# Output stores behind the next load, weight conversion in even steps, and a feed-forward activation moved to ScalarE

## The chip, the core and the metric

The kernel runs on one core of a Trainium2 chip. That core has TensorE (PE: matmuls, with PEld for its weight loads), VectorE (DVE), ScalarE (ACT), GpSimd (POOL) and SyncE (SP). SP here only issues transfers, and the core's 16 DMA engines carry them out. The metric is device time in microseconds (us), as a median of several runs; lower is better.

## The reference

Three stages follow each other: windowed attention over 4 x 8 heads of 576 positions, a mixture of 8 experts, and a feed-forward network. What the change touches belongs to the last one and to the preparation of its weights.

```python
def _moe_ref(x, w_gate, w1, w2):           # x is 2304 x 512, 8 experts, F = 1024
    ...                                    # P: gates, normalised by 8 rounds over rows and columns
    for e in range(E):
        h = np.maximum(x @ w1[e], 0.0)
        out += P[:, e:e + 1] * (h @ w2[e])

def _moe2_ref(x, w_in, w_out):             # d_ff = 2048
    h = x @ w_in
    g = np.where(h >= 1, h, np.where(h <= -1, 0.0, (h + 1) ** 2 / 4.0))
    return g @ w_out
```

The product weights w_in and w_out come as 64-bit numbers, which the kernel reads as pairs of 32-bit words and turns into fp32 itself.

## The kernel before

**Tiling.** The 2304 tokens are handled in three passes (k = 0, 1, 2) of 768 tokens. The inner width of experts and feed-forward is cut into units of 512 columns: units 0 to 15 for the experts (two an expert), 16 to 19 for the feed-forward. The main loop goes over a list of runs. A "u" run does one unit, first layer and plain second layer. An "e" run does two units, e = 4 to 7 in pass 1, e = 1 to 7 in pass 2, and e = 8 and 9, the feed-forward, in all three passes at the very end. Every fp32 product is three matmuls of high and low fp32r parts (L393).

**First layer (L398).** A 2x2 block product is done with seven block products (Strassen's scheme) in the order 1, 5, 6, 2, 7, 3, 4, each for two column groups q, so 14 steps of six matmuls. Steps 0 to 5 (blocks 1, 5, 6) are copied out of PSUM by ScalarE (L410); blocks 6 and 7 and 4 accumulate on the same bank `pa`, so block 6 waits until block 1 was copied, block 7 until the copy of block 6 is done, and block 4 until VectorE has added block 7 to its partner (L413). Each of the eight finished 128x384 tiles is given to an activation, which is a list of stages; one stage of every tile under way is issued a step.

**Second layer of an "e" run (L491).** Seven block products again, numbered n = 0 to 6 in the same order, 36 matmuls each in three steps (tiles 0, 2, 1). The sums and the high and low parts of the seven left operands are made by `Seven` while PE works, at places that the tables FIRST_WORK and SECOND_WORK give ("s" a sum, "h" a high part on ScalarE, "l" a low part on VectorE). The operands and their weights live in three buffers each, so the weights of n = 6 are loaded when n = 3 has been done with, and the next run's three first weights after n = 4, 5 and 6 (L1331 to L1336). After each step a `join` adds the product to `acc`; in the last run of each pass (e = 9) it also issues the store of a finished piece on SP, at once (L577).

**Conversion (double_steps, L212).** During passes 1 and 2 the 64-bit weights are converted in 32 pieces of 128x512: seven VectorE instructions a piece (L284 to L302, then L309 for w_in or L318 for w_out). For w_out each pair of pieces is split by `kept_pair` into high parts (ScalarE, L110), low parts (VectorE, L111) and four stores (L238); it is an iterator called `back`, advanced between the conversion's instructions by `advanced(back)`, and run to its end by `drain(back)` where its input is about to be overwritten. The parts go through two buffers called `raw2`, so a high part waits until the store two before has landed. `pull(double)` in the main loop issues one step of this generator. `at.hold` stops it before the scratch memory is needed for the next pass's input, and `at.held` says that it has stopped.

**Queues.** All transfers are issued by SP in the order of the program; an issue waits there for its semaphores, and everything behind it waits too. The program order on every engine is the order of the code.

Of the kernel before, what the change touches and what calls it, by code (L numbers as in the profile page):

```python
# [8 lines left out]
F32 = mybir.dt.float32  # L9
# [18 lines left out]
def tile_attention_moe_ffn(ctx: ExitStack, tc, q, k, v, w_gate, w1, w2, w_in, w_out, out):  # L28
# [183 lines left out]
    def double_steps(scr, stage1, stage2):  # L212
# [56 lines left out]
        for n, (u, m, c) in enumerate(pieces):  # L269
            while at.hold:  # L270
                loaded = -1
                at.held = True
                yield
            at.held = False
            if loaded < n:
                load(n)
                for _ in range(8):
                    yield
            loaded = n
            if n + 1 < len(pieces) and not at.hold:  # L280
                loaded = n + 1
                load(n + 1)
            w0, w1_ = (raws[n % 2].rearrange("p (f w) -> p f w", w=2)[:, :, i] for i in range(2))
            nc.vector.tensor_scalar(out=ai, in0=w1_, scalar1=0x7FFFFFFF, scalar2=None, op0=ALU.bitwise_and)  # L284
            yield
            nc.vector.tensor_scalar(out=a, in0=a, scalar1=F64_LO, scalar2=F64_HI, op0=ALU.max, op1=ALU.min)
            if advanced(back):
                yield
            yield
            nc.vector.tensor_scalar(out=ai, in0=ai, scalar1=3, scalar2=0x3FFFFFF8,  # L290
                                    op0=ALU.logical_shift_left, op1=ALU.bitwise_and)
            yield
            nc.vector.scalar_tensor_tensor(out=ai, in0=w1_, scalar=-0x40000000, in1=ai,
                                           op0=ALU.bitwise_and, op1=ALU.bitwise_or)
            if advanced(back):
                yield
            yield
            nc.vector.tensor_scalar(out=ti, in0=ai, scalar1=-0x800000, scalar2=None, op0=ALU.bitwise_and)
            yield
            if advanced(back):  # L300
                yield
            nc.vector.scalar_tensor_tensor(out=t, in0=w0.bitcast(U32), scalar=2.0 ** -52, in1=t,  # L302
                                           op0=ALU.mult, op1=ALU.mult)
            yield
            if m == 0:
                if c == 0:
                    drain(back)
                    raw = stage1()
                nc.vector.tensor_tensor(out=raw[:, c, :], in0=a, in1=t, op=ALU.add)  # L309
                yield  # L310
                if c == KC - 1:
                    yield from prep_w1(u, raw, lambda i: stage2().bitcast(F32R).rearrange(
                        "p h (q c f) -> p h q c f", q=UQ, c=2), 2)
            else:
                if c == 0 and u % 2 == 0:
                    raw = stage1()
                pair = [raw[:, c % 2 * 2 + i, :] for i in range(2)]
                nc.vector.tensor_tensor(out=pair[u % 2], in0=a, in1=t, op=ALU.add)  # L318
                yield
                if u % 2:  # L320
                    drain(back)
                    back = kept_pair(u // 2, c, pair)
# [158 lines left out]
    def work(ops, what):  # L481
        for x in what.split():
            {"h": ops.hi, "l": ops.low, "s": ops.sum}[x[0]](int(x[1]), int(x[2]))

    FIRST_WORK_FFN = {1: "h10 h11", 3: "l10", 4: "l11", 5: "s50", 6: "s51 h50", 8: "h51", 12: "l50", 13: "l51"}
    SECOND_WORK_FFN = {(0, 1): "s60 s61 h60", (0, 2): "h61 l60 h20", (1, 0): "l61 h21",
                       (1, 1): "l20 l21", (1, 2): "s70 s71 h70", (2, 0): "h71 l70", (2, 1): "l71",
                       (2, 2): "h30 h31", (3, 0): "l30 s40", (3, 1): "l31 s41", (3, 2): "h40 h41", (4, 0): "l40",
                       (4, 1): "l41"}

    def seven_second(finish, buf, tag):  # L491

# [74 lines left out]
    def join_plain(e, k):  # L567

        def join(o, i, x, d):
            at_ = acc[:, x, d * HD:(d + 1) * HD]  # L570
            if e == E and i in (1, 5, 6, 4):
                nc.scalar.activation(out=at_, in_=o, func=AF.Copy)
                return
            nc.vector.tensor_tensor(out=at_, in0=o, in1=at_, op=ALU.add)
            if e == E + N_PAIR - 1 and i in (2, 7, 3, 4):
                t = k * TPP + x
                nc.sync.dma_start(out=out[t * P:(t + 1) * P, d * HD:(d + 1) * HD], in_=at_)  # L577
        return join

    def act_relu(src, f, j, h_=None):  # L580
        h_ = h_ or hs
# [356 lines left out]
    def advanced(steps):  # L938
        return next(steps, steps) is not steps
# [5 lines left out]
    with tc.manual_schedule():  # L945
# [113 lines left out]
        w2o = late.tile([P, 2, KC, DM], F32R, name="w2o")  # L1059
        half = late.tile([P, 1], F32, name="half")  # L1060
        nc.vector.memset(half, 0.5)
        unity = late.tile([P, 1], F32, name="unity")
        nc.vector.memset(unity, 1.0)

        def stage1():
            return late.tile([P, KC, UF], F32, tag="raw1", bufs=1, name="raw1")
# [51 lines left out]
                return [lambda: nc.scalar.activation(out=hid[:, half_, j, f], in_=src, func=AF.Relu)]  # L1118
            return act

        at.room, at.slot = None, 0

        def act_ffn(half_):
            def act(src, f, j):
                if at.room is None:
                    at.room = stage1().rearrange("p c f -> p (c f)")
                at.slot = (at.slot + 1) % 5
                r = at.room[:, at.slot * HALF:(at.slot + 1) * HALF]

                def clamp():  # L1130
                    if f % 2 and j:
                        nc.scalar.activation(out=r, in_=src, func=AF.Relu, bias=half, scale=0.5)
                        nc.scalar.activation(out=r, in_=r, func=AF.Relu, bias=unity, scale=-1.0)
                        nc.scalar.activation(out=r, in_=r, func=AF.Square, bias=unity, scale=-1.0)
                    else:
                        nc.vector.tensor_scalar(out=r, in0=src, scalar1=-1.0, scalar2=1.0, op0=ALU.max, op1=ALU.min)
                        nc.scalar.activation(out=r, in_=r, func=AF.Square, bias=half, scale=0.5)

                return [clamp, lambda: None, lambda: nc.vector.tensor_tensor(out=hid[:, half_, j, f], in0=r, in1=src, op=ALU.max)]
            return act  # L1140

        def turn_steps(k, more, tag):
# [46 lines left out]
        for n, run in enumerate(runs):  # L1189
# [138 lines left out]
            drain(nxt)  # L1328
            for n_, t in seven_second((join_scaled if moe else join_plain)(e, k), bufs, tags[0]):
                work(ops, second_work.get((n_, t), ""))  # L1330
                if t == TPH - 1:  # L1331
                    later = n_ + 3
                    if later < len(ORDER):
                        load_op(e, ORDER[later], words(w2_buf[(ring + later) % 3]))
                    elif after and after[0] == "e":
                        load_op(after[1], ORDER[later - 7], words(w2_buf[(ring + later) % 3]))  # L1336
                if not ends and (n_, t) >= (4, 0):
                    pull(double)
                if ends and (n_, t) in ((1, 2), (2, 2), (3, 2), (4, 1), (4, 2), (5, 0), (5, 1), (5, 2), (6, 0), (6, 1)):
                    pull(build)  # L1340
            left = build
            tags.reverse()
            ring = (ring + 7) % 3
# [32 lines left out]
```

## Time and profile before

| | |
|---|---|
| Median of 3 runs | 2015.83 us (2014.94 to 2017.61) |
| The profiled execution's own time | 2012.49 us |
| Its span, first to last instruction | 2010.6 us |
| PE busy | 1967.5 us (98%) |
| DVE busy | 1468.7 us (73%) |
| ACT busy | 964.9 us (48%) |
| POOL busy | 309.2 us (15%) |
| DMA, mean over the span | 265 GB/s |

The profiled execution took 1.9 us more than its span, and 3.34 us less than the median of the runs. PE's share is an average over the whole program; what a wait costs is read where it stands. In the trace's rows a time is counted from the span's start, the second number is the duration, and a bracket at the end gives how long the engine stood idle before the row and who ended that.

### The profile page before, as it was taken

To read this page: it belongs to the slowest core of one execution; us is meant where nothing else is said; L and a number is where in the kernel's file an instruction comes from. 1 tells how busy PE (TensorE), PEld (TensorE's weight loads), DVE (VectorE), ACT (ScalarE), POOL (GpSimd) and SP (SyncE) were. 2 spreads that over 40 slices of the span, in tenths; PEclk is the share of its full clock that TensorE was granted. 3 is DMA by queue.
4 is the path that set the end of the run, shared out by engine and by line. 5 is a ranking of instruction groups with operands and counts; after the bars stand their busy time and mean duration, and the time that the engine had idled before them with its cause. 6 is when DMAs were issued, how large, how long until landed. Compare 5 with 4: busy or idle time off the path is not lost.

```text
span 2010.6 us, 33603 instructions
## 1 busy us (share of the span) xinstructions
PE 1967.5 (98%) x12602; PEld 1863.0 (93%) x12602; DVE 1468.7 (73%) x2640; ACT 964.9 (48%) x2089; POOL 309.2 (15%) x327
## 2 busy tenths in 40 slices
PE   8999999999999999999989999999999999999998
PEld 7887879898998989988989999999999999999998
DVE  6644587889988867767766576777887576986867
ACT  6555445555554443323444344444454455565554
POOL 4212214534435401011000001000000000000000
PEclk9999999999999999999999999999999999999999
DMA  7423467987788887778877868888788867787773
GB/s 177 109 67 100 180 237 279 344 312 298 297 319 315 330 308 285 280 278 309 293 272 262 278 235 331 316 284 291 291 320 320 313 248 284 241 295 267 263 250 127
DMA packets 234866, 533.07 MB, mean 265 GB/s; under 512 B 80848, under 2 KB 128464, under 8 KB 214992
## 3 DMA queue, kind: packets, MB, share of 16 engines
q1 hardware_dynamic: 234704, 530.92, 74.8%
q8 instruction: 100, 1.64, 0.3%
q14 instruction: 62, 0.51, 0.1%
HBM read 374.10 MB, written 156.76 MB: 264 GB/s over the span
## 4 chain that ended last, share of the span: by engine, by line
PE 88%; DVE 6%; DMA 3%; ACT 2%; issue 1%; SPq 0%; ACTq 0%; DVEq 0%
PE pa L395 21%; PE py L395 20%; PE pc L395 10%; PE qy L395 7%; PE qh L395 7%; PE qt L395 6%; PE pb L395 5%; PE ph L395 3%; PE qs L395 2%; PE s L747 2%; PE qx L395 1%; PE px L789 1%; PE pt L715 1%; PE pe L773 1%; DVE xf L368 1%; DMA w_sums<-raw 1%
## 5 line engine op out<-in xcount | busy, mean ns | idle before, releaser
L395 PE MATMUL pa<-xo,w1o 128*128 128x384 f32 x2736 | 516.5, 337 | 12.7 <-DVE kept L413 10.0
L395 PEld LDWEIGHTS pa<-xo,w1o 128*128 128x128 f32 x2736 | 479.4, 189 | 17.3 <-DVE kept L413 12.4
L395 PE MATMUL py<-w2o,hh 128*128 128x512 f32 x1104 | 341.6, 391 | 0.0
L395 PE MATMUL pc<-xo,w1o 128*128 128x384 f32 x1368 | 257.5, 335 | 1.8 <-DVE w1o L111 1.2
L137 POOL TENSOR_TENSOR raw<-raw 128x256 f32<-128x256 f32 x152 | 139.9, 948 | 755.1 <-DVE raw L111 275.1
L410 ACT ACTIVATE kept<-pa 128x384 f32<-128x384 f32 x228 | 110.6, 490 | 287.6 <-PE pa L395 286.6
L395 PEld LDWEIGHTS py<-w2o,hh 128*128 128x128 f32 x1104 | 207.5, 188 | 41.2
L395 PEld LDWEIGHTS pc<-xo,w1o 128*128 128x128 f32 x1368 | 238.9, 188 | 2.4 <-DVE w1o L111 1.5
L395 PE MATMUL py<-w2o,hl 128*128 128x512 f32 x552 | 215.3, 390 | 0.0
L368 DVE TENSOR_TENSOR xf<-xf 128x768 f32<-128x768 f32 x156 | 145.2, 958 | 0.8
L413 DVE TENSOR_TENSOR kept<-pb,kept 128x384 f32<-128x384 f32 x114 | 62.7, 555 | 109.3 <-PE pb L395 108.3
L111 DVE TENSOR_TENSOR w1o<-raw,w1o 128x256 fp32r<-128x256 f32 x210 | 127.7, 656 | 13.6 <-ACT w1o L110 13.3
L395 PE MATMUL pb<-xo,w1o 128*128 128x384 f32 x684 | 128.9, 335 | 0.0
L395 PEld LDWEIGHTS py<-w2o,hl 128*128 128x128 f32 x552 | 104.1, 189 | 21.7
L111 DVE TENSOR_TENSOR third<-xf,third 128x768 fp32r<-128x768 f32 (+1 forms) x110 | 105.8, 971 | 22.5 <-ACT third L110 22.3
L584 ACT ACTIVATE hh<-kept 128x384 fp32r<-128x384 f32 x138 | 72.4, 525 | 98.6 <-DVE kept L413 98.5
L395 PEld LDWEIGHTS pb<-xo,w1o 128*128 128x128 f32 x684 | 119.1, 188 | 0.0
L110 ACT ACTIVATE third<-xf 128x768 fp32r<-128x768 f32 (+1 forms) x110 | 83.9, 786 | 68.5 <-DVE xf L368 18.8
L110 ACT ACTIVATE w1o<-raw 128x256 fp32r<-128x256 f32 x210 | 77.3, 414 | 67.2 <-POOL raw L137 67.2
L1118 ACT ACTIVATE xf<-kept 128x384 f32<-128x384 f32 x132 | 67.6, 523 | 64.2 <-DVE kept L413 63.7
L585 DVE SCALAR_TENSOR_TENSOR hl<-kept,hh 128x384 fp32r<-128x384 f32 x138 | 89.6, 652 | 6.2 <-ACT hh L584 4.4
L607 DVE SCALAR_TENSOR_TENSOR acc<-py,prob,acc 128x512 f32<-128x512 f32 x120 | 84.1, 740 | 11.2 <-PE py L395 11.2
(195 smaller groups left out, 3336.7 us busy)
## 6 DMA issues: line engine op xcount, KB each, us to landing
w1o<-w_kept SPq DMA_DIRECT2D x294, 512.0 KB, 5.7
w_kept<-w1o SPq DMA_DIRECT2D x105, 512.0 KB, 4.0
w2o<-w_sums SPq DMA_DIRECT2D x48, 1024.0 KB, 5.0
w2o<-w_kept SPq DMA_DIRECT2D x46, 1024.0 KB, 5.1
w_kept<-w2o SPq DMA_DIRECT2D x26, 1024.0 KB, 7.2
w2x<-w_kept SPq DMA_DIRECT2D x21, 1024.0 KB, 4.8
w2x<-w_sums SPq DMA_DIRECT2D x20, 1024.0 KB, 4.8
w_kept<-raw SPq DMA_DIRECT2D x36, 512.0 KB, 4.5
```

Source lines behind the costliest of these rows:

```text
L110: nc.scalar.activation(out=hi, in_=raw, func=AF.Copy)
L111: return lambda: nc.vector.tensor_tensor(out=lo, in0=raw, in1=hi.bitcast(F32), op=ALU.subtract)
L137: nc.gpsimd.tensor_tensor(out=out[:, q], in0=in0[:, q], in1=in1[:, q], op=op)
L368: nc.vector.tensor_tensor(out=dst, in0=in0, in1=in1, op=ALU.subtract)
L395: nc.tensor.matmul(o, lhsT=a(h), rhs=b(l), start=first and n == 0, stop=last and n == 2, skip_group_check=on)
L410: nc.scalar.activation(out=dst, in_=src, func=AF.Copy)
L413: nc.vector.tensor_tensor(out=dst, in0=src, in1=dst, op=ALU.add)
L584: return [lambda: nc.scalar.activation(out=hi, in_=src, func=AF.Relu), lambda: nc.vector.scalar_tensor_tensor(out=lo, in0=src, scalar=0.0, ...
L585: lambda: nc.vector.scalar_tensor_tensor(out=lo, in0=src, scalar=0.0, in1=hi.bitcast(F32), op0=ALU.max, op1=ALU.subtract)]
L607: nc.vector.scalar_tensor_tensor(out=o, in0=py, scalar=prob[:, t, e:e + 1], in1=o, op0=ALU.mult, op1=ALU.add)
L747: nc.tensor.matmul(s[:, i, :], lhsT=qd[:, pr, j, :], rhs=kt[:, pr, key0(j):key0(j) + KW], start=not early, stop=not early or i == JG - 1)
L1118: return [lambda: nc.scalar.activation(out=hid[:, half_, j, f], in_=src, func=AF.Relu)]
```

## The change

Four things are changed together.

1. `join_plain` no longer issues the store of a finished output piece; it writes it down, and `send_out` issues the stores that were written down after step 1 of each of the seven products, and once at the end of the run.
2. In `double_steps` the iterator `back` is advanced at four places of a piece instead of three, each time with a step of its own, `drain(back)` before a w_in piece becomes `yield from back`, and `at.held` is set as soon as a piece has been written. In pass 2 the generator is pulled from n = 3 on instead of n = 4.
3. The feed-forward activation was, for six of eight tiles, a clamp on VectorE and a Square on ScalarE, and for two of eight three instructions on ScalarE, then a maximum on VectorE. It becomes Relu and Square on ScalarE for all eight, and one VectorE instruction with minimum and maximum.
4. The tables FIRST_WORK_FFN and SECOND_WORK_FFN place the feed-forward's sums and parts at other steps.

```diff
@@ double_steps
             nc.vector.tensor_scalar(out=ai, in0=w1_, scalar1=0x7FFFFFFF, scalar2=None, op0=ALU.bitwise_and)
+            if advanced(back):
+                yield
             yield
...
             if m == 0:
                 if c == 0:
-                    drain(back)
+                    yield from back
                     raw = stage1()
                 nc.vector.tensor_tensor(out=raw[:, c, :], in0=a, in1=t, op=ALU.add)
+                at.held = at.hold
                 yield
...
-    FIRST_WORK_FFN = {1: "h10 h11", 3: "l10", 4: "l11", 5: "s50", 6: "s51 h50", 8: "h51", 12: "l50", 13: "l51"}
+    FIRST_WORK_FFN = {1: "h10 h11", 2: "l10 l11", 3: "s50", 4: "s51 h50 h51", 6: "l50", 7: "l51"}
...
@@ join_plain
             if e == E + N_PAIR - 1 and i in (2, 7, 3, 4):
-                t = k * TPP + x
-                nc.sync.dma_start(out=out[t * P:(t + 1) * P, d * HD:(d + 1) * HD], in_=at_)
+                at.done.append((k * TPP + x, d, at_))
         return join
+
+    def send_out():
+        for t, d, from_ in at.done:
+            nc.sync.dma_start(out=out[t * P:(t + 1) * P, d * HD:(d + 1) * HD], in_=from_)
+        at.done.clear()
...
@@ act_ffn
-                def clamp():
-                    if f % 2 and j:
-                        nc.scalar.activation(out=r, in_=src, func=AF.Relu, bias=half, scale=0.5)
-                        nc.scalar.activation(out=r, in_=r, func=AF.Relu, bias=unity, scale=-1.0)
-                        nc.scalar.activation(out=r, in_=r, func=AF.Square, bias=unity, scale=-1.0)
-                    else:
-                        nc.vector.tensor_scalar(out=r, in0=src, scalar1=-1.0, scalar2=1.0, op0=ALU.max, op1=ALU.min)
-                        nc.scalar.activation(out=r, in_=r, func=AF.Square, bias=half, scale=0.5)
-
-                return [clamp, lambda: None, lambda: nc.vector.tensor_tensor(out=hid[:, half_, j, f], in0=r, in1=src, op=ALU.max)]
+                def squared():
+                    nc.scalar.activation(out=r, in_=src, func=AF.Relu, bias=half, scale=0.5)
+                    nc.scalar.activation(out=r, in_=r, func=AF.Square)
+
+                return [squared, lambda: None,
+                        lambda: nc.vector.scalar_tensor_tensor(out=hid[:, half_, j, f], in0=r, scalar=1.0, in1=src,
+                                                               op0=ALU.min, op1=ALU.max)]
...
@@ main loop, second layer of an "e" run
                 work(ops, second_work.get((n_, t), ""))
+                if t == 1:
+                    send_out()
                 if t == TPH - 1:
                     later = n_ + 3
...
-                if not ends and (n_, t) >= (4, 0):
+                if not ends and n_ >= (4 if k < 2 else 3):
                     pull(double)
...
+            send_out()
             left = build
```

Three places show how the order moves. The first is VectorE's program around the border of pass 1's runs e = 4 and e = 5 and the first layer of e = 5: L111 on `raw` is a low part of the conversion, L309 the first w_in piece, L413 the first layer's addition. Before:

```order
L563 SCALAR_TENSOR_TENSOR acc<-qh,prob,acc 128x256 x3
L290 TENSOR_SCALAR xf<-xf 128x512
L293 SCALAR_TENSOR_TENSOR xf<-xf 128x512
L111 TENSOR_TENSOR raw_9711<-raw_8672,raw_9711 128x2x256
L298 TENSOR_SCALAR xf<-xf 128x512
L302 SCALAR_TENSOR_TENSOR xf<-xf 128x512
L111 TENSOR_TENSOR raw_9788<-raw_8672,raw_9788 128x256
L111 TENSOR_TENSOR raw_9812<-raw_8672,raw_9812 128x2x256
L111 TENSOR_TENSOR raw_9816<-raw_8672,raw_9816 128x2x256
L309 TENSOR_TENSOR raw_9820<-xf 128x512
L413 TENSOR_TENSOR kept_9748<-pb_9744,kept_9748 128x384
L413 TENSOR_TENSOR kept_9749<-pb_9745,kept_9749 128x384
```

With the change, at the same place of PE's order (L566 is the join that was L563, L417 the addition that was L413):

```order
L566 SCALAR_TENSOR_TENSOR acc<-qh,prob,acc 128x256 x3
L302 TENSOR_SCALAR xf<-xf 128x512
L304 SCALAR_TENSOR_TENSOR xf<-xf 128x512
L321 TENSOR_TENSOR raw_8670<-xf 128x512
L284 TENSOR_SCALAR xf<-xf 128x512
L288 TENSOR_SCALAR xf<-xf 128x512
L111 TENSOR_TENSOR raw_9770<-raw_8670,raw_9770 128x2x256
L417 TENSOR_TENSOR kept_9738<-pb_9734,kept_9738 128x384
L417 TENSOR_TENSOR kept_9739<-pb_9735,kept_9739 128x384
```

Three low parts in a row, each behind a high part that waits for a buffer, and L309 stood ahead of the additions; one low part is left there, and the others follow in later steps.

The second is SP's program at the border of pass 1's last "u" run and e = 4: L238 is a store of converted weights, L263 a load of raw 64-bit weights, L188 the loads of second-layer weights for e = 4, L171 those of first-layer weights. Before:

```order
L238 DMA w_sums_128<-raw_9082 128x2x512
L238 DMA w_sums_128<-raw_9110 128x2x512
L263 DMA xf<-in_moe_w_out_dram 128x1024
L238 DMA w_kept_118<-raw_9120 128x2x512
L188 DMA w2x<-w_kept_109 128x2048
L188 DMA w2o<-w_sums_124 128x2048 x2
L171 DMA w1o_70<-w_kept_90 128x1024
```

With the change:

```order
L238 DMA w_sums_128<-raw_9074 128x2x512
L238 DMA w_sums_128<-raw_9094 128x2x512
L263 DMA xf<-in_moe_w_out_dram 128x1024
L188 DMA w2x<-w_kept_109 128x2048
L188 DMA w2o<-w_sums_124 128x2048 x2
L171 DMA w1o_70<-w_kept_90 128x1024
L238 DMA w_kept_118<-raw_9129 128x2x512
```

The store that stood ahead of the three second-layer loads now stands behind them and behind one load of first-layer weights.

The third is SP's program in pass 0's run e = 9, at the products n = 3 to 5; L577 and L584 are the stores of finished output, the first L188 after them the load for n = 6. Before:

```order
L188 DMA w2o<-w_sums_129 128x2048
L577 DMA out_dram<-acc 128x256 x3
L188 DMA w2o<-w_kept_120 128x2048
L577 DMA out_dram<-acc 128x256 x3
L188 DMA w2x<-w_kept_117 128x2048
```

With the change:

```order
L188 DMA w2o<-w_sums_129 128x2048
L584 DMA out_dram<-acc 128x256 x2
L188 DMA w2o<-w_kept_120 128x2048
L584 DMA out_dram<-acc 128x256 x3
L188 DMA w2x<-w_kept_117 128x2048
```

The third store of n = 3 has moved behind the load for n = 6; the two stores before it are still ahead of that load.

## Rows read from the trace of the kernel before

**Rows 1.** Timeline of PE, 900 to 1060 us: start, us, what, [idle before, releaser]

```profile
917.82 2.36 PE L395 MATMUL pa<-xo,w1o 128*128 128x384 f32 x12 [1.87 <-DVE kept L413]
...
936.33 2.27 PE L395 MATMUL pa<-xo,w1o 128*128 128x384 f32 x12
...
953.71 3.71 PE L395 MATMUL pa<-xo,w1o 128*128 128x384 f32 x12 [2.63 <-DMA w1o<-w_kept]
957.22 2.52 PE L395 MATMUL pc<-xo,w1o 128*128 128x384 f32 x12
...
1019.16 5.99 PE L395 MATMUL pa<-xo,w1o 128*128 128x384 f32 x24 [6.37 <-DVE kept L413]
```

**Rows 2.** A window of 50 us: length, PE, PEld, DVE, ACT, POOL busy, granted clock, DMA

```profile
1000.00:1050.00 50.00, 43.63 (x276) 43.31 (x275) 30.26 (x50) 22.85 (x42) 2.22 (x3) 0.93 0.82 291
```

**Rows 3.** Chain of waits, 900 to 1060 us: start, us, what

```profile
907.22 8.34 DMA w_sums<-raw
...
1006.99 8.53 DMA w_kept<-raw
...
1015.63 0.64 ACT raw L110
...
1017.63 1.49 DVE kept L413 x3
```

**Rows 4.** Timeline of SP's issues, 930 to 960 us

```profile
940.37 0.36 SPq L238 DMA_DIRECT2D w_kept<-raw  x1
940.78 0.46 SPq L188 DMA_DIRECT2D w2x<-w_kept  x1
...
942.62 1.65 SPq L171 DMA_DIRECT2D w1o<-w_kept  x3
```

**Rows 5.** Timeline of PE in the feed-forward runs

```profile
1712.11 4.32 PE L395 MATMUL pa<-xo,w1o 128*128 128x384 f32 x24
...
1738.13 4.49 PE L395 MATMUL qh<-w2o,hh 128*128 128x256 f32 x34 [0.35 <-DVE hh L111]
...
1757.70 4.54 PE L395 MATMUL qh<-w2o,hl 128*128 128x256 f32 x36 [2.16 <-DMA w2o<-w_kept]
...
1879.77 5.87 PE L395 MATMUL qh<-w2o,hh 128*128 128x256 f32 x36 [2.42 <-DMA w2o<-w_kept]
...
2002.88 4.54 PE L395 MATMUL qh<-w2x,third 128*128 128x256 f32 x36 [2.10 <-DMA w2x<-w_kept]
```

**Rows 6.** Timelines of SP and of DVE in pass 0's run e = 9

```profile
1749.31 2.73 SPq L577 DMA_DIRECT2D out_dram<-acc  x3
1752.14 0.37 SPq L188 DMA_DIRECT2D w2o<-w_kept  x1
...
1748.87 0.75 DVE L574 TENSOR_TENSOR acc<-qs,acc 128x256 f32<-128x256 f32 x2
...
1751.27 0.41 DVE L574 TENSOR_TENSOR acc<-qx,acc 128x256 f32<-128x256 f32 x1
```

**Rows 7.** Groups by line, 1640 to 2011 us: count | busy, mean ns | idle before

```profile
L1137 ACT ACTIVATE raw<-raw,half 128x384 f32<-128x384 f32 x72 | 42.9, 612 | 32.1 <-DVE raw L1136 31.1
L110 ACT ACTIVATE hh<-xf 128x768 fp32r<-128x768 f32 x28 | 22.9, 841 | 17.0 <-DVE xf L368 12.2 <-PE qh L395 3.4 <-PE qx L395 1.2
L410 ACT ACTIVATE kept<-pa 128x384 f32<-128x384 f32 x47 | 22.2, 488 | 24.3 <-PE pa L395 24.3
L1132 ACT ACTIVATE raw<-kept,half 128x384 f32<-128x384 f32 x24 | 14.5, 605 | 2.3 <-DVE kept L413 2.2
...
L1139 DVE TENSOR_TENSOR xf<-raw,kept 128x384 f32<-128x384 f32 x72 | 39.6, 551 | 6.7 <-ACT raw L1134 6.5
...
L1136 DVE TENSOR_SCALAR raw<-kept 128x384 f32<-128x384 f32 x48 | 17.3, 360 | 1.7
```

**Rows 8.** Timeline of ACT in pass 0's run e = 9

```profile
1725.54 0.62 ACT L1133 ACTIVATE raw<-raw,unity 128x384 f32<-128x384 f32 x1
1726.19 0.62 ACT L1134 ACTIVATE raw<-raw,unity 128x384 f32<-128x384 f32 x1
```

More of the change, by code (lines that the diff above doesn't have):

```diff
@@ L291, in double_steps @@
                                     op0=ALU.logical_shift_left, op1=ALU.bitwise_and)
+            if advanced(back):
+                yield
             yield
@@ L299, in double_steps @@
             yield
-            if advanced(back):
-                yield
             nc.vector.scalar_tensor_tensor(out=t, in0=w0.bitcast(U32), scalar=2.0 ** -52, in1=t,
@@ L318, in double_steps @@
                 nc.vector.tensor_tensor(out=pair[u % 2], in0=a, in1=t, op=ALU.add)
+                at.held = at.hold
                 yield
@@ L483, in work @@
             {"h": ops.hi, "l": ops.low, "s": ops.sum}[x[0]](int(x[1]), int(x[2]))
-    FIRST_WORK_FFN = {1: "h10 h11", 3: "l10", 4: "l11", 5: "s50", 6: "s51 h50", 8: "h51", 12: "l50", 13: "l51"}
[L486 to L489, printed above, removed]
+    FIRST_WORK_FFN = {1: "h10 h11", 2: "l10 l11", 3: "s50", 4: "s51 h50 h51", 6: "l50", 7: "l51"}
+    SECOND_WORK_FFN = {(0, 0): "s60 s61 h60 h61", (0, 1): "l60 l61", (1, 0): "h20 h21", (1, 1): "l20 l21",
+                       (1, 2): "s70", (2, 0): "s71 h70 h71", (2, 1): "l70 l71", (3, 0): "h30 h31",
+                       (3, 1): "l30 l31", (3, 2): "s40", (4, 0): "s41 h40 h41", (4, 1): "l40 l41"}
     def seven_second(finish, buf, tag):
@@ L1061, in tile_attention_moe_ffn @@
         nc.vector.memset(half, 0.5)
-        unity = late.tile([P, 1], F32, name="unity")
-        nc.vector.memset(unity, 1.0)
         def stage1():
@@ L1119, in act_kept @@
             return act
-        at.room, at.slot = None, 0
+        at.room, at.slot, at.done = None, 0, []
         def act_ffn(half_):
```

## The prediction

> **What bounds the kernel.** I read four views in this order: the page's busy shares, the timeline of PE in stretches of 60 us (only rows with idle time ahead of them), the chain of waits around the longest of these, and the timelines of SP and DVE at the same places. PE is busy 98% of the span. So the time is PE's own work, which the change leaves as it is, plus the places where PE waits. After the first 280 us, in attention and the gates, which the change doesn't reach, there are few. In pass 1 there are three [rows 1]: 1.87 us and 6.37 us for VectorE's addition `kept`, and 2.63 us for first-layer weights. In the feed-forward each of the three e = 9 runs has one of 2.16, 2.42 or 2.10 us for the weights of n = 6, and one of about 0.35 us for a low part ahead of n = 2 [rows 5], of which one of three is shown.
>
> A wait costs more than its idle time where the clock falls after it. Twelve matmuls take 2.27 us at 936, but 3.71 and 2.52 us just behind the wait of 2.63; twenty-four take 4.32 us, but 5.99 us behind that of 6.37 [rows 1, 5]. The granted clock of the window with this wait is 0.93, and PE works 43.63 of its 50 us [rows 2], so part of it ran at 1.2 instead of 2.4 GHz. Behind 2.42 us the 36 matmuls took 5.87 us; behind 2.16 us they took 4.54 [rows 5].
>
> **The change part by part.** *Conversion.* The wait of 6.37 us is made by the drained `back`. In the chain [rows 3] a store needs 8.53 us to land, only then does ScalarE write the next high part into that buffer (1015.63), then VectorE makes the low part, and only then come the additions (1017.63) for which PE waits. In the changed order one low part is left ahead of the additions, its high part was issued a step before, and the store whose buffer it takes stands a product earlier in the run, over 10 us before. So the wait goes: 6.37 + (5.99 - 4.32) = 8.0 us. The 1.87 us at 917.82 [rows 1] have the same cause, with a store that took 8.34 us to land [rows 3] while two steps of `back` met at one place; now each has its own, and the buffer's store is issued some 6 us ahead of the high part: 1.9 us.
>
> What is late next? All conversion instructions remain, but low parts now stand between the conversion's steps. At the border of the last "u" run and e = 4 four high parts follow stores that are only 6 to 8 us older (PE's time between the two places). If such a store lands after 8.3 to 8.5 us, as those of [rows 3] did, instead of soon enough, VectorE is held 1 to 2 us. An addition has some 3 us before PE misses it: three steps of six matmuls lie between, and four such steps take 4.32 us [rows 5]. I take nothing, and keep 4 us for it as a bound: two such waits of 1.9.
>
> *The weights at 953.71.* SP issued the store of a low part at 940.37, then the second-layer loads from 940.78, and the first-layer load for which PE waited at 942.62 [rows 4]; it took 11.1 us to land, behind three megabytes. PE was done with the buffers of the second-layer weights when e = 4 began, at 936.33 [rows 1]. In the change that store stands behind these loads. The raw load ahead of them waits only for a conversion instruction which, by its place, VectorE does by about 936 (an estimate). So the loads start some 4 us earlier, and the first-layer load, which waits for PE's first block, is issued at 936.33 + 2.27 = 938.6 and, with the same 11.1 us, lands by 949.7, while PE needs it 14 steps after 936.33, at about 951. That gains 2.63 + 1.44 + 0.25 (what the two slow rows have over 2.27) = 4.3 us. Were the loads no earlier, the gain would be nothing.
>
> *Stores.* In the e = 9 run the third store waited for VectorE's join of qx, which ended at 1751.7, and the load for n = 6 was issued at 1752.14 [rows 6]; PE waited for it until 1757.70. In the change the load stands behind the two stores of qs alone, whose joins ended at 1749.6. That alone makes it 2.1 us earlier, just about the wait. VectorE is also less late by then: the second layer has six clamps of 0.36 to 0.55 us fewer ahead of it (L1136), and two low parts and two sums of the old order stand behind those joins now. I take 4 us earlier in all, so that the wait goes in all three passes: 2.16 + 2.42 + 2.10 + (5.87 - 4.54) = 8.0 us. The earlier parts of n = 2 take the waits of 0.35: 1.0 us.
>
> *Activation.* VectorE's part of a tile is one instruction of a maximum's size, 0.551 us [rows 7], as before, and the clamp is gone. ScalarE gets two instructions for each of eight tiles. The first is L1132's form, 605 ns. A dependent one starts 0.65 us after it [rows 8]. The second, a Square without a bias tile, isn't in the trace; it lies between a Copy without one (L410, 488 ns) and a Square with one (L1137, 612 ns). A tile then costs ScalarE 0.65 + 0.4 = 1.05 us with the overlap that neighbours show, 1.14 without it, and 1.26 with the long Square. I take 1.1, nearest to the Copy, whose operands are alike.
>
> The Trainium skill, "ScalarE: Activation LUTs", section "What ACT_TABLE_LOAD costs", gives 186 ns + 0.833 ns a column for immediates and 93 ns more for a bias tile; by that estimate the Square takes 506 ns and a tile 1.06 us.
>
> Over the two first layers of a run ScalarE then has 16 x 1.1 tiles, 12 copies of 0.49 and up to 7 high parts of 0.84 us [rows 7], 29.4 us, and PE 28 steps, which at a quarter of 4.32 us less the overlap of rows are some 29.1 us. That is level, so ScalarE ends a few us late, where the second layer leaves it room. The narrow place is the second copy of block 6: it now stands behind both high parts of operand 5, which wait for VectorE's sums. By adding the durations in order it ends 0.1 to 0.8 us before PE wants to add block 7. With 1.26 us a tile it would be up to 1 us late in each of six runs. I take 0.5 us in all, from nothing to 6 us.
>
> *Nothing else pays.* The end of the program keeps one store behind the last join. The conversion ends within pass 2's e = 6 as before, so no drain comes due. Pass 2 shows no wait of a microsecond, and three more instructions in n = 3 lie beside PE's 36 matmuls there.
>
> Sum: 8.0 + 1.9 + 4.3 + 8.0 + 1.0 - 0.5 = 22.7 us. The profiled execution took 2012.49 us (span 2010.6 and 1.9 around it) and would take 1989.8; the median of the runs is 3.34 us above it, so 1993.
>
> **Rivals.** *The loads stay late.* If VectorE's lag in e = 9 or the DMA queues make the loads as late as before, the 4.3 and 8.0 us stay: 1993 + 12.3 = 2005, or with one of the two about 2000. For it: the wait is cured by 2.1 us from the order alone, and a load of 1 MB needs 5.4 us or more with stores around it. Against it: VectorE's work ahead is less.
>
> *Store landings hold the spread conversion.* The waits of 1.9 and 6.4 us come back at the new places as two to four of 2 us each, one with a slow clock: about 8 us, 2001. For it: landings of 8.3 and 8.5 us. Against it: these two fell where several stores were in flight together.
>
> *ScalarE becomes the bound of the feed-forward (slower).* If a tile costs p us there, two first layers cost 16p + 11.8 us. The gain of 23 us is gone when each of six runs loses 3.9 us, that is from p = 1.32 on if nothing of the lag is absorbed, and at p = 1.6 six runs lose 8.3 us each: 1993 + 50 = 2043, slower than before. Against it: p over 1.26 needs waits that no row shows, and the second layer absorbs some us a run. The Trainium skill, same page, section "Rules for kernel authors", gives maximum and minimum to VectorE and not ScalarE; the clamp's 0.36 us against 0.605 us for the Relu that takes its place agrees.
>
> *No change.* The waits turn up elsewhere in full, since no engine's work falls by much: within 4 us of 2015.8. For it: PE is held by two slower engines in turn. Against it: both are idle a quarter of the time or more where PE waits.
>
> **How the numbers follow.** The forecast has 0.58, the late loads 0.16, the landings 0.12, ScalarE 0.06, no change 0.08. The best case adds the wait of 0.6 us in pass 2 and the pipeline's gap at each wait, some 3 us: 1990. For the upper end I take late loads with some of the landings: 2007. This holds about 0.8. The forecast's own range is 1989 to 1999. Four us, 0.2%, is what can be told from no change. Faster: 0.58 + 0.16 + 0.12, less 0.01: 0.85; same 0.09; slower 0.06.
>
> **What would show it.** Right: PE's rows at the first layers of pass 1's e = 4 and e = 5 and its last "u" run have no idle time over 0.5 us, the granted clock of that stretch is 1.00, n = 6 in each e = 9 run starts without a wait, ScalarE's Square takes about 0.5 us and no wait of PE names `kept` L414, the copy. Wrong: a wait of PE for ScalarE in the feed-forward, or for `kept` behind a low part of the conversion, or the load of n = 6 still landing behind PE.

## The result, and the profile after

The changed kernel takes 1985.33 us (median of four runs, 1984.10 to 1990.27), and the kernel before, on the same chip, 2016.72 (2014.94 to 2017.74). The ratio is 0.985, with a 95% interval of 0.9831 to 0.9869. The forecast was 1993 with a range of 1989 to 2007, so the direction was right and the gain too small: 31.4 us measured, 23 to 24 forecast.

The first and the fourth part of the page of the changed kernel: busy time of each engine, and the chain of waits.

```profile
PE 1957.6 (99%) x12602; PEld 1855.8 (94%) x12602; DVE 1436.8 (72%) x2567; ACT 982.9 (50%) x2137; POOL 312.5 (16%) x327
...
PE 94%; DVE 3%; ACT 2%; DMA 1%; issue 0%; SPq 0%; DVEq 0%; ACTq 0%
```

The three places of [rows 1] in the timeline of PE after the change:

```profile
915.91 2.24 PE L399 MATMUL pa<-xo,w1o 128*128 128x384 f32 x12
...
934.31 2.27 PE L399 MATMUL pa<-xo,w1o 128*128 128x384 f32 x12
...
946.81 4.61 PE L399 MATMUL pa<-xo,w1o 128*128 128x384 f32 x24
951.25 2.27 PE L399 MATMUL pc<-xo,w1o 128*128 128x384 f32 x12
...
1006.41 4.32 PE L399 MATMUL pa<-xo,w1o 128*128 128x384 f32 x24
```

None has idle time ahead of it, and 24 matmuls at 1006.41 take 4.32 us, where [rows 1] had 5.99 behind a wait of 6.37. The window of [rows 2] is full (same columns):

```profile
1000.00:1050.00 50.00, 50.00 (x360) 50.00 (x360) 36.69 (x59) 23.32 (x40) 1.43 (x2) 1.00 0.81 283
```

SP's issues ahead of e = 4, which answer to [rows 4]. Before, the store (L238) of 940.37 stood ahead of the second-layer loads (L188) and held them until 940.78, though the raw load (L263) had been issued at 936.48. Now they begin at 934.92, right behind the raw load, and the store stands behind them:

```profile
934.52 0.35 SPq L263 DMA_DIRECT2D xf<-in_moe_w_out_dram  x1
934.92 0.43 SPq L188 DMA_DIRECT2D w2x<-w_kept  x1
935.44 0.85 SPq L188 DMA_DIRECT2D w2o<-w_sums  x2
936.61 0.32 SPq L171 DMA_DIRECT2D w1o<-w_kept  x1
937.84 0.37 SPq L238 DMA_DIRECT2D w_kept<-raw  x1
```

In the feed-forward run e = 9 of pass 0, timelines of SP, DVE and PE (which answer to [rows 5, 6]): VectorE's joins of qs follow PE at once, the load for n = 6 is issued right behind their two stores, and PE starts n = 6 at 1738.14 with no wait. Nor is there a wait at n = 2 (1720.91), where [rows 5] had 0.35 us. What is left of idle time is 0.22 us in the next run, e = 8, and 0.21 in the e = 8 run after that, for a copy of ScalarE. SP, DVE and PE in this order:

```profile
1728.75 0.81 SPq L584 DMA_DIRECT2D out_dram<-acc  x2
1729.72 0.33 SPq L188 DMA_DIRECT2D w2o<-w_kept  x1
```

```profile
1728.30 0.76 DVE L577 TENSOR_TENSOR acc<-qs,acc 128x256 f32<-128x256 f32 x2 [0.28 <-PE qs L399]
```

```profile
1720.91 4.46 PE L399 MATMUL qh<-w2o,hh 128*128 128x256 f32 x36
...
1733.84 4.46 PE L399 MATMUL qt<-w2o,hh 128*128 128x256 f32 x36
1738.14 4.48 PE L399 MATMUL qh<-w2o,hl 128*128 128x256 f32 x36
...
1766.80 1.33 PE L399 MATMUL pa<-xo,w1o 128*128 128x384 f32 x6 [0.22 <-ACT kept L414]
```

ScalarE in the feed-forward, grouped by line (count, busy us, mean ns, idle before), and then one tile after another in its timeline. These answer to [rows 7, 8]:

```profile
L1137 ACT ACTIVATE raw<-raw 128x384 f32<-128x384 f32 x96 | 50.5, 526 | 3.0
L1136 ACT ACTIVATE raw<-kept,half 128x384 f32<-128x384 f32 x72 | 43.5, 605 | 8.3 <-DVE kept L417 7.9
```

```profile
1754.62 0.53 ACT L1137 ACTIVATE raw<-raw 128x384 f32<-128x384 f32 x1
1755.05 0.60 ACT L1136 ACTIVATE raw<-kept,half 128x384 f32<-128x384 f32 x1
1755.69 0.53 ACT L1137 ACTIVATE raw<-raw 128x384 f32<-128x384 f32 x1
1756.12 0.60 ACT L1136 ACTIVATE raw<-kept,half 128x384 f32<-128x384 f32 x1
```

A tile costs ScalarE 1.07 us (1755.05 to 1756.12), against 1.1 taken.

**Where the time went.** PE is the bound, so its time between the same matmuls of two kernels shows what a stretch gained. Two marks cut the span in three: PE's first product with `ident,acc` at about 717 us, and its first one after the passes. Before, then after:

```profile
716.67 0.38 PE L1150 MATMUL p<-ident,acc 128*128 128x128 f32 x2
...
1639.34 0.49 PE L1150 MATMUL p<-ident,acc 128*128 128x128 f32 x3
```

```profile
716.85 0.38 PE L1152 MATMUL p<-ident,acc 128*128 128x128 f32 x2
...
1622.78 0.49 PE L1152 MATMUL p<-ident,acc 128*128 128x128 f32 x3
```

With spans of 2010.6 and 1984.4 us the stretches are 716.67, 922.67 and 371.26 us before, and 716.85, 905.93 and 361.62 after: the passes gain 16.7, the feed-forward 9.6, the start nothing. Between the same matmuls inside the passes, the last "u" run of pass 1 gains 2.15, e = 4 4.2, e = 5 8.2 and pass 2 2.1.

### The profile page after: what moved, and what is told of

Its sections match the earlier page's. It is cut to its first block, busy times and chain, and to the rows that moved or that the text cites. A ratio compares the mean times of both kernels' runs of the same rounds, so it can differ in the third digit from the quotient of the medians.

```text
span 1984.4 us, 33637 instructions
## 1 busy us (share of the span) xinstructions
PE 1957.6 (99%) x12602; PEld 1855.8 (94%) x12602; DVE 1436.8 (72%) x2567; ACT 982.9 (50%) x2137; POOL 312.5 (16%) x327
## 4 chain that ended last, share of the span: by engine, by line
PE 94%; DVE 3%; ACT 2%; DMA 1%; issue 0%; SPq 0%; DVEq 0%; ACTq 0%
PE pa L399 22%; PE py L399 21%; PE pc L399 11%; PE qh L399 8%; PE qt L399 7%; PE qy L399 7%; PE pb L399 5%; PE ph L399 3%; PE qs L399 2%; PE s L754 2%; PE qx L399 1%; PE px L796 1%; PE pt L722 1%; PE pe L780 1%; PE pg L887 0%; DMA big<-in_q_dram 0%
## 5 line engine op out<-in xcount | busy, mean ns | idle before, releaser
L414 ACT ACTIVATE kept<-pa 128x384 f32<-128x384 f32 x228 | 110.8, 490 | 294.6 <-PE pa L399 293.5
L417 DVE TENSOR_TENSOR kept<-pb,kept 128x384 f32<-128x384 f32 x114 | 62.8, 556 | 105.4 <-PE pb L399 105.1
L111 DVE TENSOR_TENSOR w1o<-raw,w1o 128x256 fp32r<-128x256 f32 x210 | 117.6, 605 | 17.7 <-ACT w1o L110 17.5
L111 DVE TENSOR_TENSOR third<-xf,third 128x768 fp32r<-128x768 f32 (+1 forms) x110 | 101.2, 934 | 19.9 <-ACT third L110 19.8
L110 ACT ACTIVATE hh<-xf 128x768 fp32r<-128x768 f32 x78 | 63.3, 841 | 61.0 <-DVE xf L372 26.4
```

The source lines that it names most:

```text
L110: nc.scalar.activation(out=hi, in_=raw, func=AF.Copy)
L111: return lambda: nc.vector.tensor_tensor(out=lo, in0=raw, in1=hi.bitcast(F32), op=ALU.subtract)
L414: nc.scalar.activation(out=dst, in_=src, func=AF.Copy)
L417: nc.vector.tensor_tensor(out=dst, in0=src, in1=dst, op=ALU.add)
```

## The experiments

Twelve kernels, in three groups, each group on one chip beside runs of the kernel before (2015.33 to 2016.16 us). "Passes" and "feed-forward" are the stretches above, in each kernel's profiled execution.

| Kernel | median us | ratio, interval | start | passes | feed-forward |
|---|---|---|---|---|---|
| before, the first profile | 2015.83 | | 716.67 | 922.67 | 371.26 |
| before again (e4) | 2016.0 | 0.9994, 0.998 to 1.0007 | 723.58 | 924.94 | 373.38 |
| conversion alone (e1) | 1995.79 | 0.9891, 0.9876 to 0.9905 | 716.48 | 907.46 | 372.96 |
| stores alone (e2) | 2006.16 | 0.9949, 0.9936 to 0.9961 | 717.64 | 925.56 | 363.30 |
| activation and order (e3) | 2006.82 | 0.9951, 0.9936 to 0.9967 | 716.50 | 926.51 | 361.29 |
| order alone (e7) | 2006.41 | 0.9956, 0.994 to 0.9971 | 719.26 | 923.35 | 360.69 |
| activation alone (e10) | 2006.48 | 0.9952, 0.9935 to 0.9969 | 715.36 | 924.05 | 365.49 |
| stores, activation, order (e5) | 2003.19 | 0.9942, 0.9927 to 0.9957 | 719.04 | 926.82 | 361.34 |
| all three (after) | 1985.33 | 0.985, 0.9831 to 0.9869 | 716.85 | 905.93 | 361.62 |
| after, drain kept (e6) | 1985.95 | 0.9853, 0.9838 to 0.9868 | 716.54 | 908.05 | 361.61 |
| after, old activation (e9) | 1986.95 | 0.9853, 0.9837 to 0.987 | 717.36 | 905.91 | 361.13 |
| after, old stores (e11) | 1985.48 | 0.985, 0.9832 to 0.9869 | 714.87 | 906.18 | 361.75 |
| after, h51 later (e12) | 1986.14 | 0.9849, 0.9832 to 0.9865 | 715.66 | 908.07 | 360.67 |
| after, third ScalarE step (e8) | 2031.49 | 1.0086, 1.0057 to 1.0116 | 715.40 | 907.92 | 407.38 |

**The change in its parts.** e1 is the kernel before with the conversion's hunks of the diff (with `at.held` and the `pull` line), e2 with `send_out` and its calls, e3 with `squared` and both tables. e4 is the kernel before, unchanged.

> Of the four changes only the one to the conversion (back advanced evenly, at.held early, pass 2 pulled from n = 3). If the terms simply add, its trace loses the three waits of pass 1 (8.2, 4.3 and 2.1 us) and some 1.5 us in pass 2, and keeps the feed-forward's waits of 2.1 to 2.4 us: a ratio to the kernel before of 0.992 (16 us). If the runs of the kernel before lie 4 us above its first profile because its pass 1 waits vary, the gain in the runs is 19 to 21 us, 0.990. If the waits only move, it is under 8 us.

> Only the output stores are issued later. Theory: the order alone makes the load of n = 6 some 2.1 us earlier, so the waits of 2.1 to 2.4 us in the three e = 9 runs shrink to under 0.5 us and the clock drop behind one of them goes; the 0.35 us ahead of n = 2 stay: 6 to 8 us, ratio 0.9965. Rival: VectorE's lag sets the load's time and the stores of qs hold it as long: under 3 us, ratio 0.9985 or above.

> Only the activation and the two feed-forward tables. Theory: VectorE comes earlier to the joins, so the stores are released earlier and the load for n = 6 with them, though a store still stands ahead: the waits of 2.1 to 2.4 us shrink to 0.5 to 1.5 us, those of 0.35 us go, and 0.2 us come in for the copy L414 in the e = 8 runs: 3 to 6 us, ratio 0.998. Rival: all of the gain in the feed-forward comes from here (8 us, 0.996) or none (under 1 us).

> The kernel before, unchanged, for another execution's trace. If its executions differ by the waits of pass 1 and the feed-forward, its waits ahead of PE differ from 1.87, 2.63 and 6.37 us (pass 1) and 2.16, 2.42 and 2.10 us (feed-forward) by more than 1 us in sum, and a run with a longer span shows it there or in a lower clock; if they differ in attention, the first 280 us are longer or shorter by that much and the rest is the same.

The conversion alone gains 1.1%, or 20.4 us, and all of it in the passes. That is the second of e1's three texts, in which the runs of the kernel before lie above its first profile. Its waits at n = 6 stay, and one of 1.36 us for first-layer weights is left, as PE's timeline in e1 shows:

```profile
952.36 2.32 PE L399 MATMUL pc<-xo,w1o 128*128 128x384 f32 x12 [1.36 <-DMA w1o<-w_kept]
...
1742.34 5.90 PE L399 MATMUL qh<-w2o,hl 128*128 128x256 f32 x35 [2.22 <-DMA w2o<-w_kept]
```

Stores alone and activation with order alone each gain 0.5%, and all of it in the feed-forward. That is 10.0 and 9.3 us, more than either theory gave (6 to 8, and 3 to 6). Each takes away the same waits at n = 6. The kernel before, taken again, has the waits of the first profile in other sizes: 3.57, 2.15 and 6.68 us in pass 1, and 2.52, 2.47 and 2.23 at n = 6. Its start took 6.9 us longer as well. Its timeline of PE at e = 5:

```profile
1027.57 7.28 PE L395 MATMUL pa<-xo,w1o 128*128 128x384 f32 x24 [6.68 <-DVE kept L413]
```

**Do the gains in the feed-forward add up?** e5 is the changed kernel with the conversion's hunks undone. e11 undoes the stores alone:

```diff
-                at.done.append((k * TPP + x, d, at_))
+                t = k * TPP + x
+                nc.sync.dma_start(out=out[t * P:(t + 1) * P, d * HD:(d + 1) * HD], in_=at_)
...
-                if t == 1:
-                    send_out()
...
-            send_out()
```

> The changed kernel with the conversion's steps of before: stores behind the loads, the new activation and its order of parts stay. Theory (overlap): the stores and the activation each remove the same wait, that of the e = 9 runs for the weights of n = 6, so both together are worth what one is, 10 to 11 us: 2005 to 2007 us; pass 1 keeps waits of about 1.9 to 4, 2 to 2.6 and 5.5 to 6.7 us, and n = 6 has none. Rival (the gains add up): 2016.7 - 10.6 - 9.9 = 1996. Rival (the third part is worth what is left of the whole, 31.4 - 20.9): also 2006, which agrees with the first.

> The changed kernel with the output stores issued at the joins, ahead of the next load, as before. Theory (overlap: the order of the parts already lets the load land in time): no wait at n = 6, 1984 to 1988 us. Rival (the stores hold a share of the gain of their own): waits of 0.5 to 2 us at n = 6 and 1990 to 1995.

They don't. Stores and activation together gain 12.1 us (0.58%) and not the sum of some 19. The feed-forward takes 361.34 us, as with the activation and order alone, and with the old stores the whole change is as fast as with the new ones (e11). e5 keeps all three waits of pass 1:

```profile
922.12 3.67 PE L395 MATMUL pa<-xo,w1o 128*128 128x384 f32 x12 [3.81 <-DVE kept L413]
...
960.40 4.21 PE L395 MATMUL pa<-xo,w1o 128*128 128x384 f32 x12 [3.70 <-DMA w1o<-w_kept]
...
1025.89 6.68 PE L395 MATMUL pa<-xo,w1o 128*128 128x384 f32 x24 [5.46 <-DVE kept L413]
```

**Order or activation?** e7 is the kernel before with the two new tables FIRST_WORK_FFN and SECOND_WORK_FFN alone, e10 with `squared` alone, e9 the changed kernel with `clamp` in the place of `squared`.

> The kernel before with the two new tables alone, which say at which steps of a feed-forward run the high parts, low parts and sums are made. Theory (the removed clamps relieve VectorE): the three waits of 0.35 us ahead of n = 2 go, those of 2.1 to 2.5 us for the weights of n = 6 stay in two or three passes, at 1 to 2.5 us: 2012 to 2016. Rival (the order of the parts relieves VectorE at its joins): the waits at n = 6 go as well and the time is that of the activation with its tables, 2005 to 2008.

> The kernel before with the new activation alone, the order of the parts as before. Theory (either of the two relieves VectorE enough): no wait over 0.7 us at n = 6, the three of 0.35 us ahead of n = 2 stay, 2006 to 2010 us. Rival (the order does it all): the waits of 2.1 to 2.5 us at n = 6 stay, 2013 to 2017.

> The changed kernel with the activation of before (VectorE's clamps, or three ScalarE steps), the new order of parts, stores and conversion stay. Theory (the order of the parts, not the cheaper activation, relieves VectorE at the joins): 1984 to 1987 us as with the new activation, no wait at n = 6, and the waits of 0.2 us for the second copy of block 6 go, since ScalarE has less to do. Rival (the clamps make VectorE late again): waits of 0.5 us and more in the feed-forward, 1988 to 1995.

For e7 my theory fell: the order of the parts alone takes away every wait of the feed-forward, 360.69 us. In e10 neither text was right about the waits. Those at n = 6 shrink, to 1.65, 1.61 and 1.18 us, and those ahead of n = 2 go: 365.49 us. The medians (2006.48 and 2006.41 us) don't tell e10 from e7; only the traces do. In e9 the old activation with the new order gives 361.13 us, with no wait of 0.2 us in the feed-forward. So the order alone is enough, and with it the new activation adds nothing that the runs show.

What decides at n = 6 is when the load is issued against PE's start of the product before (qt). In [rows 6] the load is issued at 1752.14, 1.05 us after qt's start in the same profile, PE's timeline of before:

```profile
1751.09 4.46 PE L395 MATMUL qt<-w2o,hh 128*128 128x256 f32 x36
```

SP's and then PE's timeline of e10:

```profile
1747.94 2.73 SPq L577 DMA_DIRECT2D out_dram<-acc  x3
1750.78 0.37 SPq L188 DMA_DIRECT2D w2o<-w_kept  x1
```

```profile
1750.52 4.46 PE L395 MATMUL qt<-w2o,hh 128*128 128x256 f32 x36
...
1756.63 4.55 PE L395 MATMUL qh<-w2o,hl 128*128 128x256 f32 x36 [1.65 <-DMA w2o<-w_kept]
```

The same two of e7:

```profile
1749.01 2.73 SPq L576 DMA_DIRECT2D out_dram<-acc  x3
1751.84 0.37 SPq L188 DMA_DIRECT2D w2o<-w_kept  x1
```

```profile
1753.51 4.46 PE L395 MATMUL qt<-w2o,hh 128*128 128x256 f32 x36
```

e10 issues 0.3 us after qt's start and waits 1.65; e7 issues 1.7 us before it, behind the same three stores, and waits for nothing. With the stores alone (e2) it was 0.9 us before (load at 1754.07, qt at 1754.93), also without a wait that the rows show; in the changed kernel it is 4.1 us before (1729.72, 1733.84). Whatever brings the load forward by some 2 us takes the whole wait, and a second such edit finds nothing left.

**Spread or drain?** e6 is the changed kernel with one line of before:

```diff
-                    yield from back
+                    drain(back)
```

> The changed kernel with one line of before: ahead of the first piece's addition the remaining steps of the other operand's preparation are drained and not spread. Theory (the spread alone cures the wait): by then only one low part is left to drain, whose high part was made a step before, so PE's wait for kept at the first layer of pass 1's e = 5 stays under 0.5 us and the time is 1985 to 1988. Rival (the drain made the wait): the wait of 5.5 to 6.7 us comes back with its slow matmuls, 1993 to 1997.

No wait comes back at e = 5, as PE's timeline of e6 shows:

```profile
1007.63 4.32 PE L399 MATMUL pa<-xo,w1o 128*128 128x384 f32 x24
```

So the rest of the conversion's change cures the wait, and the drain was only the place where it showed. That the steps' even spread does it, and not the earlier `at.held`, is argued: the two weren't run apart. The passes take 2 us more here than after. Most of that is two waits of 0.72 and 0.56 us for first-layer weights at 949 to 952 us, which e12 (0.46 and 1.18) and e8 (0.36 and 1.30) have too with the changed line: those loads land just in time, in some executions a little late.

**ScalarE as the bound.** e8 adds one line to the changed kernel:

```diff
                     nc.scalar.activation(out=r, in_=r, func=AF.Square)
+                    nc.scalar.activation(out=r, in_=r, func=AF.Copy)
```

> The changed kernel with a third ScalarE instruction for each tile of the feed-forward's activation, a copy in place, which computes nothing new. Theory (the rival of the prediction in which ScalarE becomes the bound has the right formula): a tile then costs 1.07 + 0.5 = about 1.55 us, two first layers 16 x 1.55 + 11.8 = 36.6 us against PE's 29.1, so PE waits some 7.5 us in each of six runs, and more where the clock falls: 1985 + 45 = 2030, with 2020 to 2040 as bounds. Rival (the second layer absorbs it): waits of 1 to 3 us a run, 1990 to 2003.

2031.49 us, 46 slower than the changed kernel and inside the bounds that the rival's formula gave. Timelines of ACT and PE in e8 and a window of it (columns of [rows 2]): a tile now costs ScalarE 1.62 us, and PE waits for its copy of block 6 in every run, by 2.5 to 3.4 us. In five of the six the 12 matmuls behind it take 3.6 to 3.9 us for 2.3. Those shown here take 3.91, at a granted clock of 0.56, so most of them ran at 1.2 GHz:

```profile
1703.49 0.60 ACT L1136 ACTIVATE raw<-kept,half 128x384 f32<-128x384 f32 x1
...
1705.11 0.60 ACT L1136 ACTIVATE raw<-kept,half 128x384 f32<-128x384 f32 x1
```

```profile
1713.66 3.91 PE L399 MATMUL pa<-xo,w1o 128*128 128x384 f32 x12 [2.68 <-ACT kept L414]
```

```profile
1713.66:1717.57 3.91, 3.91 (x13) 3.91 (x14) 2.97 (x5) 3.02 (x7) 0.00 (x0) 0.56 0.22 88
```

**A version with nothing left to wait for.** e12 moves one high part a step later in FIRST_WORK_FFN:

```diff
-... 4: "s51 h50 h51", 6: "l50", 7: "l51"}
+... 4: "s51 h50", 5: "h51", 6: "l50", 7: "l51"}
```

> The changed kernel with one high part of operand 5 made a step later, behind ScalarE's copy of block 6. Theory (the copy stands behind a high part that waits for VectorE): the two or three waits of PE of 0.2 us for that copy go and nothing new comes, 0.4 to 0.7 us less in the profiled span, which the runs can't tell from none: 1983.5 to 1986. Rival (the later high part makes its low part and n = 5 late): new waits of 0.3 us and more, 1986 to 1990.

The waits of 0.2 us go, and the feed-forward is 0.95 us shorter than after (360.67 against 361.62). That is not to be told from no change in the runs. e6, e9, e11, e12 and the changed kernel agree within their intervals, and none of them is shown to beat it.

## Why the prediction was right and wrong

**Right: the places and causes.** Every wait named went in the changed kernel's profile. The conversion's two: no idle time at the matching rows, and e1 shows that they went with the conversion alone. The weights at 953: against PE's start of e = 4 the loads are issued 3.8 us earlier (940.78 - 936.33 before, 934.92 - 934.31 after), some 4 were taken, and 4.2 us gained of 4.3. In five of the seven profiles with the new conversion, though, waits of 0.3 to 1.4 us for these weights are left. At n = 6 the load is 5 us earlier against PE (1.05 us after qt's start, then 4.1 before), 4 taken. The price p = 1.1 us of a tile on ScalarE was 1.07. The Square without a bias tile took 526 ns, against "about 0.5". The estimate of 506 ns from the Trainium skill, "ScalarE: Activation LUTs", section "What ACT_TABLE_LOAD costs", is 20 ns short of that; the bounds from the rows (488 to 612) held it. The narrow place was also the right one: PE's wait for the copy of block 6 behind both high parts is the one left in the feed-forward, 0.22 and 0.21 us, where the forecast had the copy 0.1 to 0.8 us early. By the prediction's own signs this counts against it, for it asked that "no wait of PE names `kept` L414, the copy".

**Right: the slower rival's formula.** 16p + 11.8 us with p = 1.62 is 37.7 us, 8.6 over PE's 29.1, or 52 us over six runs. Measured were 45.8 (407.38 - 361.62).

**Wrong: the size.** The profiled execution came to 1986.27 us where 1989.8 was forecast, and the median lies 0.9 us below the profiled time where it was put 3.3 above. The miss of 7.7 us has these two halves.

*The sum, 3.5 us short: 26.2 us measured between the two profiles, 22.7 forecast.* The largest part is pass 2: "Pass 2 shows no wait of a microsecond" was priced at nothing, and 2.1 us came from several small ones there, of which two have a row, 0.22 and 0.64 us. The feed-forward gave 9.6 for 8.5. The three waits of 0.35 us, priced at their idle time, 1.0, gave 2.3 between the same matmuls, for the matmuls behind such a wait are slow too: 34 take 4.49 us in [rows 5], and all 36 take 4.46 without the wait. The waits at n = 6 gave 8.7 for 8.0, and the activation cost 1.0 and not 0.5, in the two waits of 0.2 us and behind them. The conversion gave 2.15 and 8.2 for 1.9 and 8.0. So what the sum left out is mostly the cost of a wait beyond its idle time. The prediction knew it ("the pipeline's gap at each wait"), but put it into its best case alone.

*The step that failed most: "the median of the runs is 3.34 us above it, so 1993".* It takes what other executions have on top of the profiled one as a constant that the change leaves alone. Most of it was in the very waits that the change removes. Seven profiled executions have the conversion of before: their passes take 922.67 to 926.82 us, mean 924.8, and the execution that the forecast was made from is the shortest, 2.2 us under the mean. Seven have the new one: 905.9 to 908.1, mean 907.1. So the passes gain 17.8 us in the mean, where 14.2 were forecast. The three executions with the old stores, order and activation take 371.26, 373.38 and 372.96 us in the feed-forward, and again the forecast's own is the shortest, 1.3 us under the mean; against 361.6 the mean gives 10.9, where 8.5 were forecast. The two together, 3.4 us, are about the 3.34 that the forecast added. That its execution was the mildest was luck; that the distance would outlive the waits was the error.

The term that carries most of it is the first place of [rows 1]. It was put at 1.9 us, from a wait of 1.87 with hardly a slow matmul behind it. The same place shows waits of 2.83 to 4.01 us in the other six profiles. In e5 the 12 matmuls behind the wait of 3.81 took 3.67 us, so there it costs 5.2. Between the same matmuls, mean of the seven old profiles against mean of the seven new, the place gave 4.8 us for 1.9. The place at e = 5, put at 8.0, was sized better: 5.46 + (6.68 - 4.32) = 7.8 in e5, 6.68 + (7.28 - 4.32) = 9.6 in e4, and 8.6 in the mean. Pass 2 gave 1.4 for nothing. The weights at 953 gave 2.9 for 4.3, since part of their wait is left in five of the new seven: the 4.2 us of the first pair of profiles were a good draw.

Why is it longer there? In e5 the chain of waits shows the same links as [rows 3], a store that must land before ScalarE's high part, but the store is issued later:

```profile
910.00 0.96 SPq L171
...
911.07 8.79 DMA w_sums<-raw
...
922.12 3.67 PE pa L395 x12
```

SP's issues ahead of it, in the first profile of before and then in e5, tell why:

```profile
905.57 0.70 SPq L171 DMA_DIRECT2D w1o<-w_kept  x1
907.22 0.38 SPq L238 DMA_DIRECT2D w_sums<-raw  x1
```

```profile
907.94 3.03 SPq L171 DMA_DIRECT2D w1o<-w_kept  x1
911.07 0.66 SPq L238 DMA_DIRECT2D w_sums<-raw  x1
```

The store stands in SP's order behind a first-layer load (L171), which SP holds until PE has read the buffer. In the first profile SP was done with that load before the store's data was there. In e5 it held the store. Against the moment when PE is ready (its start less its wait) the store is issued 8.73 us ahead in the first profile and 7.24 in e5, and it lands after 8.34 and 8.79 us: 1.49 + 0.45 is the whole difference of the two waits, 3.81 - 1.87. The chains of e2, e3 and e10 go through the same issue of L171, with landings of 8.69, 8.76 and 8.73. In e4 and e7 the chain goes through VectorE and not SP; there the store is issued 7.57 and 8.27 us ahead and lands after 8.89 and 8.84. So the forecast read the mechanism of this place rightly and its size from the mildest execution.

The mean gains of the two stretches, 17.8 and 10.9, make 28.7 us of the 31.4. The interval of the ratio leaves 26 to 34 for the whole, so the runs don't say whether there is a rest.

**Wrong: what the activation is for.** The forecast counted "six clamps of 0.36 to 0.55 us fewer" as what makes VectorE less late at the joins, beside the order. By the traces of e7, e9 and e10 the order alone is enough and the clamps alone are not. With the order in place, e9's ScalarE and VectorE split the work as before and PE doesn't notice. The Trainium skill, "ScalarE: Activation LUTs", section "Rules for kernel authors", puts maximum and minimum on VectorE. A single instruction agrees (360 ns for the clamp, 605 for the Relu, [rows 7]); the kernel's time shows neither gain nor loss from it: 1986.95 us with the clamps, 1985.33 without, intervals overlapping.

**The other rivals.** Late loads and store landings didn't come: no kernel with the new conversion has a wait at e = 5 or at the first place of [rows 1], and of the kernels with the new stores or the new order none shows a wait for the weights of n = 6 in an e = 9 run. What is left of late loads are the waits of up to 1.4 us at 948 to 952.

## What to carry to other kernels

A wait read in one profiled execution is one draw: before it becomes a term, look at the same place in a second execution, and do not add the distance from the profile to the median as a constant, for the waits that a change removes are part of it. Where several edits aim at one wait, find by how much the late load or result must come earlier, and count that wait once; here any of three edits brought the load forward enough or nearly so. Work on an engine that PE isn't waiting for can be reordered rather than made cheaper, but its price per tile is worth knowing, since one more instruction a tile there cost 46 us.

## What the runs showed of the hardware

- The same wait, behind code that is the same up to there, differs between executions, 1.87 to 4.01 us at one place and 5.33 to 6.93 at another, as do the slow matmuls behind it. At the first place, in four of six executions, the difference goes mostly back to a load that SP held ahead of the store; why the second place differs is not shown.
- The clock also falls where nothing was changed. In e4 the granted clock of the stretch from 20 to 80 us was 0.72, where the first profile of the same kernel had 0.94. Both lie between the levels of 1.2 and 2.4 GHz, so PE ran at each of them for a part. The start took 723.58 us for 716.67. Windows of e4 and of the first profile, same columns as above:

```profile
20.00:80.00 60.00, 54.30 (x450) 47.35 (x450) 35.81 (x104) 32.98 (x142) 21.52 (x29) 0.72 0.61 139
```

```profile
20.00:80.00 60.00, 54.32 (x551) 47.56 (x551) 42.76 (x124) 39.99 (x173) 23.39 (x31) 0.94 0.66 153
```

- A ScalarE instruction in place behind another that writes the same tile adds 0.55 us to a tile (1.07 to 1.62 in e8), hardly more than its own 525 ns.
